# Fused linear-attention and gated-MLP layer: six of the 22 feature tiles of the MLP form their block sums on VectorE instead of by copies into PSUM

## The chip, the core and the metric

One core of a Trainium2 chip runs the whole layer in one launch. The metric is the device time of an execution in microseconds (us), and the lower the better. A kernel's figure is the median of its timed executions; beside it stands one profiled execution, whose trace has the start and duration of every instruction on every engine: TensorE (PE, with its weight loads as PEld), VectorE (DVE), ScalarE (ACT), GpSimd (POOL), and the queues that issue transfers, above all that of SyncE (SP).

## What is computed

The input is x, 2048 tokens of 512 values in float32. After a layer norm, a linear-attention branch and a ReLU-gated MLP branch both read the normalized tokens, and the output joins them. Cut to what matters:

```python
def _B_ref(x, W_gate, W_up, W_down):          # D = 512, F = 1376
    gate = jnp.einsum("bsd,df->bsf", x, W_gate)
    up = jnp.einsum("bsd,df->bsf", x, W_up)
    gate = gate * (gate > 0)
    h = gate * up
    return jnp.einsum("bsf,fd->bsd", h, W_down)

xn = _layernorm(x, axis=-1)
s = _A_ref(xn, A_wqkv, A_w_phi, A_wo)         # 32 heads, feature map by two softmaxes, linear attention
g = _silu(_B_ref(xn, B_W_gate, B_W_up, B_W_down))
return x + s * g
```

The change lies in `gate` and `up` and in how `h` is formed from them.

## The kernel before, in words

**Order of work.** A first phase normalizes and transposes the tokens, projects keys, values and queries and gathers the attention state; it ends at about 167 us of the profile. The rest is two halves. Each half takes 1024 tokens as two blocks of 512, and runs a loop over NF = 11 feature tiles `f` of 128 gate and 128 up features each (line 1203). For each tile `gate_up` (line 559) forms `h` of both blocks, transposed, as 128 features by 512 tokens. `down` (line 633) multiplies `h` by W_down, two tiles at a time (CHUNKS, line 27), and after the last tile come the rest of the down products and the output tiles (`out_tile`, line 896).

**Precision.** Every product of two float32 blocks is made of three matmuls on a high part and a low part of each operand (`mm3`, line 199). With two contraction steps of 128 a product is six matmuls of 128x512 here. `split` (line 194) makes the parts: ScalarE rounds the high part (`hh`), GpSimd subtracts for the low part (`hl`).

**Seven products for eight.** The 2x2 blocks of the tokens are block by contraction half (A11, A12 of the first block, A21, A22 of the second), those of the weights contraction half by gate and up. Winograd's form of Strassen's product needs seven products of sums of blocks. The sums of the tokens (S1 to S4) lie ready in `XT`, those of the weights in `wa`, `wb`, `wc`, `wd`. Call the products P1 = A11·wa0, P2 = A12·wa1, P3 = S4·wd, P4 = A22·wc1, P5 = S1·wc0, P6 = S2·wb0, P7 = S3·wb1. Then the four results are

- gate of the first block: P1 + P2, up of the first block: P1 + P6 + P5 + P3,
- gate of the second block: P1 + P6 + P7 + P4, up of the second block: P1 + P6 + P7 + P5.

**How gate_up adds them.** It issues P1, P7, P6, P2, P5, P4, P3. Sums that share products are carried on in PSUM: ScalarE copies P1 from bank `pa` into bank `pb` (line 565), and TensorE accumulates P6 on top of the copy (line 574); ScalarE copies that sum from `pb` into bank `pd` (line 578), and TensorE accumulates P5 on it (line 588). VectorE adds P7, which ScalarE has copied to `t7`, into `pb` (line 579), forms the second block's up from `pd` and `t7` (line 590), and the two products of gate and up (lines 596 and 601). So P5 can't begin before ScalarE's second copy, and P3 can't begin before VectorE has read `pd` in line 590. After each of the seven products the function yields.

**What stands between the products.** `run` (line 1181) drives the generator. At its second, fourth, sixth and seventh yield (DOWNS, line 41) it issues one step of a pending `down`, if there is one: six or nine matmuls. There is none in tiles 0 and 1 of a half, since the first pair of tiles isn't done, and none in tile 10, since `drain()` (line 1215) has issued the rest ahead of it. In tiles 2 to 9 there always is.

**What sets the order of other work.** `Clock` (line 63) is a planner that lives in the recording of the program: `pace.pump()` issues background work (preparing weights, `q_pair` of the attention queries, which uses VectorE, ScalarE and GpSimd) where its modelled engine times say that it fits. The order recorded is the order on each engine's queue, and each queue is worked off in order. Tiles come from pools: 8 PSUM banks for everything, and 41 buffers of 2 KB for each partition (`u2`) for weights, loads and temporaries; a new tile waits for the last user of the buffer it gets.

**Transfers.** `used(c)` (line 1225) reloads a token block of `XT` for the second half, in the last tile of the first half, as soon as the product that read it is issued. `halfway` reloads `wc`, `wd` and the down weights of the next tile after the third product.

All of the recorded operations carry the line of a helper (L59 in the profile), so the groups are told apart by the names of their tiles: `pa`, `pb`, `pc`, `pd` are the PSUM banks of gate_up; the profile writes `t` for `t7`.

Of the kernel before, what the change touches and what calls it, by code (L numbers as in the profile page):

```python
# [8 lines left out]
F32R = mybir.dt.float32r  # L9
AF = mybir.ActivationFunctionType  # L10
ALU = mybir.AluOpType
AX = mybir.AxisListType

P = 128
# [7 lines left out]
BT = 512  # L22
# [20 lines left out]
A21, A22, A11, A12, S1, S2, S3, S4 = range(8)  # L43
# [116 lines left out]
def layer_kernel(ctx: ExitStack, tc: tile.TileContext, x, wkT, wqT, wv, wo, wf, cst, out):  # L160
    pace = Clock()
    nc = InOrder(tc, pace)
# [4 lines left out]
    def ps(shape=(P, 512), name="ps"):  # L167
        return pp.tile(list(shape), F32, tag="ps", name=name)
# [7 lines left out]
    def u2(shape, name, dt=F32):  # L176
        return sb.tile(list(shape), dt, tag="u2", bufs=B2, name=name)
# [7 lines left out]
    def f32(t):  # L185
        return t.bitcast(F32)

    def add(engine, o, a, b, op=ALU.add):
        engine.tensor_tensor(o, a, b, op=op)

    def mm(o, w, m, start, stop):
        nc.tensor.matmul(o, w, m, start=start, stop=stop, skip_group_check=True)

    def split(hi, lo, src, lo_engine=None):

        nc.scalar.activation(hi, src, AF.Copy)
        add(lo_engine or nc.vector, lo, src, f32(hi), ALU.subtract)

    def mm3(ps_out, w, m, ks, first=True, last=True):

        n = len(ks)
        for i, k in enumerate(ks):
            (wh, wl), (mh, ml) = w(k), m(k)
            mm(ps_out, wl, mh, first and i == 0, False)
            mm(ps_out, wh, ml, False, False)
            mm(ps_out, wh, mh, False, last and i == n - 1)
            if i < n - 1:
                pace.pump()
# [238 lines left out]
    RAW, FT, WD = {}, {}, {}  # L447
# [21 lines left out]
    def w_pair(name):  # L469
        return u2((P, 2, 2, P), name, F32R), u2((P, 2, 2, P), name, F32R)  # L470
# [68 lines left out]
    def f_reload(f, part):  # L539
        if part == 0:  # L540
            FT[f] = [w_pair("wa"), w_pair("wb"), None, None]
            for i, t in enumerate([*FT[f][0], *FT[f][1]]):
                nc.sync.dma_start(f32(flat3(t)), wspill[f][i])
            return
        FT[f][2:] = w_pair("wc"), u2((P, 2, 2, P), "wd", F32R)
        WD[f] = u2((P, D), "fdh", F32R), u2((P, D), "fdl", F32R)
        for i, t in enumerate([*FT[f][2], FT[f][3], *WD[f]]):
            nc.sync.dma_start(f32(flat3(t)), wspill[f][4 + i])

    def w_of(f, i, c=None):  # L550
        t = FT[f][i]
        if c is None:
            return lambda k: (t[:, 0, k, :], t[:, 1, k, :])
        return lambda k: (t[0][:, c, k, :], t[1][:, c, k, :])

    def a_of(c):
        return lambda k: (XT[:, c, 0, k, :], XT[:, c, 1, k, :])

    def gate_up(f, used, halfway):

        pa = ps(name="pa")
        mm3(pa, w_of(f, 0, 0), a_of(A11), range(2))
        used(A11)
        pb = ps(name="pb")
        nc.scalar.activation(pb, pa, AF.Copy)
        last_split()
        yield
        pc = ps(name="pc")
        mm3(pc, w_of(f, 1, 1), a_of(S3), range(2))
        used(S3)  # L570
        t7 = u2((P, BT), "t7")
        nc.scalar.activation(t7, pc, AF.Copy)
        yield
        mm3(pb, w_of(f, 1, 0), a_of(S2), range(2), first=False)
        FT[f][1] = None
        used(S2)
        pd = ps(name="pd")
        nc.scalar.activation(pd, pb, AF.Copy)
        add(nc.vector, pb, pb, t7)
        halfway()  # L580
        yield
        mm3(pa, w_of(f, 0, 1), a_of(A12), range(2), first=False)
        FT[f][0] = None
        used(A12)
        r = u2((P, BT), "r")
        nc.scalar.activation(r, pa, AF.Relu)
        yield
        mm3(pd, w_of(f, 2, 0), a_of(S1), range(2), first=False)
        used(S1)
        add(nc.vector, t7, pd, t7)  # L590
        yield
        mm3(pb, w_of(f, 2, 1), a_of(A22), range(2), first=False)
        FT[f][2] = None
        used(A22)
        h1 = u2((P, BT), "hh", F32R), u2((P, BT), "hl", F32R)
        nc.vector.scalar_tensor_tensor(t7, pb, 0.0, t7, op0=ALU.max, op1=ALU.mult)
        split(*h1, t7, nc.gpsimd)
        yield
        mm3(pd, w_of(f, 3), a_of(S4), range(2), first=False)
        used(S4)  # L600
        add(nc.vector, r, pd, r, ALU.mult)
        h0 = u2((P, BT), "hh", F32R), u2((P, BT), "hl", F32R)
        LATE.append(lambda: split(*h0, r, nc.gpsimd))
        FT.pop(f)
        HS[f] = [h0, h1]
        yield

    HS, Y, LATE = {}, {}, []

    def last_split():  # L610
        while LATE:
            LATE.pop()()
# [566 lines left out]
    pending = []  # L1179

    def run(g, per=1):
        n = 0
        for _ in g:
            pace.pump()
            n += 1
            for _ in range(DOWNS.get(n, 0)):
                if not pending:
                    break
                if next(pending[0], pending) is pending:
                    pending.pop(0)  # L1190
                    if pending:
                        next(pending[0])
                pace.pump()
# [7 lines left out]
    for half in range(2):  # L1201
        b0, b1 = 2 * half, 2 * half + 1
        for f in range(NF):
            if half == 0:
                at[0] = N + f
                pace.finish(preps, lambda: f in DONE)
                if f == 0:
                    queries = pace.add(all_queries(0), 20)
            if half == 1 and f == 0:
                queries = pace.add(all_queries(1), 5)  # L1210
            again = f + 1 < NF and (half or f + 1 in AHEAD)
            if again and f + 1 not in FT:
                f_reload(f + 1, 0)
            if f == NF - 1:
                drain()
                pace.finish(queries)
                for q in QUERIES[half][:4]:
                    if q not in LOADED:
                        o_load(q)
                WO = wo_load()  # L1220
            if f == NF - 2 and not half:
                for q in QUERIES[half][:2]:
                    o_load(q)

            def used(c):
                if half == 0 and f == NF - 1:
                    nc.sync.dma_start(f32(XT[:, c]), xt_spill[:, c - 1])
            run(gate_up(f, used, lambda: again and f_reload(f + 1, 1)))
            for c, fs in enumerate(CHUNKS[:-1]):
                if f == fs[-1]:  # L1230
                    pending.extend(down((b0, b1)[j], j, fs, c == 0) for j in (1, 0))

        last_split()
        drain()
        if half == 0:
            f_reload(0, 0)
            f_reload(0, 1)
        fs = CHUNKS[-1]
        for j, b in enumerate((b1, b0)):
            j = 1 - j  # L1240
            if b == b0:
                for q in QUERIES[half][:2]:
                    o_split(q)
            parts = {}
            for i in range(TPB):
                if j == 1 and i < 3:
                    parts[i] = ps(name="py")
                    down_rows(parts[i], i, j, fs[:-1], True, False)
                    pace.pump()
            for i in range(TPB):  # L1250
                if i in parts:
                    down_rows(parts[i], i, j, fs[-1:], False, True)
                else:
                    parts[i] = ps(name="py")
                    down_rows(parts[i], i, j, fs, True, True)
                y_sum(b, i, parts[i], False, True)
                y = Y[b][:, i, :]
                nc.scalar.activation(y, y, AF.Silu)
                if b * TPB + i in yspill:
                    pace.when(y, lambda t=b * TPB + i, y=y: nc.sync.dma_start(yspill[t], y))  # L1260
                pace.pump()
        for g in fs:
            HS.pop(g), WD.pop(g)
        qs = QUERIES[half]
        for m, q in enumerate(qs):
            if half == 0 and m == 1:
                f_reload(1, 0)
            if m + 2 < len(qs):
                o_split(qs[m + 2])
            if m + 4 < len(qs):  # L1270
                o_load(qs[m + 4])
            for j in range(2):
                out_tile(2 * q + j, WO)
                pace.pump()
# [56 lines left out]
```

## Time and profile before

| | before |
|---|---|
| median of three executions | 564.98 us (564.98 to 565.27) |
| profiled execution | 565.71 us, of which the span of the trace 563.9 us |
| TensorE busy in the span | 556.8 us, 2618 matmuls |
| VectorE, ScalarE, GpSimd busy | 373.4, 312.8, 404.6 us |
| gate_up in tiles 0 and 1, first half | 167.5 to 189.7 us |
| gate_up in tile 10, first half | 315.0 to 324.5 us |
| gate_up in tiles 0 and 1, second half | 357.1 to 377.7 us |
| gate_up in tile 10, second half | 504.6 to 515.4 us |

The profile's matmul rows overlap: a row lasts some 0.39 us, and the next begins before it is over. So TensorE's pace is read from the starts of successive groups of rows, not from durations.

### The profile page before, as it was taken

The numbers are of one execution on the slowest core, as the hardware profiler recorded it, in microseconds if no ns is written. First come the engines' busy times: TensorE is split into PE (matmuls) and PEld (weight loads), VectorE is DVE, ScalarE is ACT, GpSimd is POOL, SyncE is SP. The second block draws the span as 40 slices with busy tenths as digits, with TensorE's granted clock in tenths as the row PEclk, the third lists the DMA queues.
The fourth block names the chain that finished last, engine by engine and source line by source line (L and its number), as shares of the span: only waits on it lengthen the run. The fifth ranks groups of instructions, "written<-read, shape, count | busy, mean of one in ns | idle before, by whom it ended". The sixth has DMA issues, their size and how long they took to land.

```text
span 563.9 us, 8200 instructions
## 1 busy us (share of the span) xinstructions
PE 556.8 (99%) x2618; PEld 465.7 (83%) x2618; DVE 373.4 (66%) x566; ACT 312.8 (55%) x561; POOL 404.6 (72%) x347
## 2 busy tenths in 40 slices
PE   9999999999999999999999999999999999999997
PEld 8898888888888788888888888788888888888886
DVE  5878867677654797699953332679683958764323
ACT  3898787775546567456464251345455555645610
POOL 1689987999888377997988343464568786878473
PEclk9999999999999999999999999999999999999999
DMA  8349989956599817978779999992656765559974
GB/s 271 144 133 260 257 256 305 271 155 176 149 297 317 309 62 263 337 260 293 261 249 341 313 388 410 377 392 57 194 186 200 244 205 158 178 180 314 254 208 166
DMA packets 84539, 137.98 MB, mean 245 GB/s; under 512 B 7824, under 2 KB 34320, under 8 KB 83600
## 3 DMA queue, kind: packets, MB, share of 16 engines
q1 hardware_dynamic: 81040, 125.33, 64.6%
q0 software_dynamic: 3312, 12.06, 11.2%
q8 instruction: 21, 0.34, 0.2%
q14 instruction: 22, 0.18, 0.1%
q10 hardware_dynamic: 144, 0.07, 0.0%
HBM read 76.87 MB, written 52.69 MB: 230 GB/s over the span
## 4 chain that ended last, share of the span: by engine, by line
PE 92%; DVE 3%; DMA 2%; ACT 1%; issue 1%; POOL 0%; SPq 0%; DVEq 0%; ACTq 0%
PE py L59 21%; PE pd L59 10%; PE pa L59 10%; PE pb L59 10%; PE pq L59 8%; PE pso L59 8%; PE pv L59 7%; PE pk L59 7%; PE pc L59 5%; PE pkv L59 3%; PE pnum L59 2%; DMA wvr<-wv 2%; PE pxT L59 1%; DVE eq L59 1%; DMA xt<-x 1%
## 5 line engine op out<-in xcount | busy, mean ns | idle before, releaser
L59 PE MATMUL py<-fdh,hl 128*128 128x512 f32 x176 | 68.5, 389 | 0.0
L59 PE MATMUL py<-fdl,hh 128*128 128x512 f32 x176 | 68.5, 389 | 0.0
L59 PE MATMUL py<-fdh,hh 128*128 128x512 f32 x176 | 68.5, 389 | 0.0
L59 PE MATMUL pa<-XT,wa 128*128 128x512 f32 x264 | 67.2, 389 | 0.0
L59 POOL TENSOR_TENSOR hl<-t,hh 128x512 fp32r<-128x512 f32 x22 | 28.5, 1295 | 50.9 <-ACT hh L59 49.9
L59 PEld LDWEIGHTS pa<-XT,wa 128*128 128x128 f32 x264 | 49.5, 188 | 10.2
L59 DVE TENSOR_TENSOR y<-py,y 128x512 f32<-128x512 f32 x40 | 27.5, 689 | 37.8 <-PE py L59 37.8
L59 DVE TENSOR_TENSOR pb<-pb,t 128x512 f32<-128x512 f32 x22 | 15.3, 697 | 45.9 <-ACT pd L59 45.9
L59 ACT ACTIVATE hh<-t 128x512 fp32r<-128x512 f32 x22 | 13.9, 633 | 53.6 <-DVE t L59 53.6
L59 PE MATMUL pv<-wvh,XT 128*128 128x512 f32 x128 | 43.5, 401 | 0.0
L59 POOL TENSOR_TENSOR phl<-ek,phl 128x1024 fp32r<-128x1024 f32 x15 | 36.1, 2403 | 10.4 <-ACT phl L59 10.4
L59 PE MATMUL pk<-wkh,XT 128*128 128x512 f32 x128 | 42.4, 392 | 0.0
L59 POOL TENSOR_TENSOR ez<-eq,zB 128x1024 f32<-128x1024 f32 x16 | 38.7, 2421 | 3.4 <-ACT eq L59 2.3
L59 PE MATMUL pq<-XT,wqh 128*128 128x512 f32 (+1 forms) x144 | 40.3, 366 | 0.0
L59 POOL TENSOR_TENSOR hl<-r,hh 128x512 fp32r<-128x512 f32 x22 | 28.4, 1292 | 16.1 <-ACT hh L59 14.4
L59 PEld LDWEIGHTS py<-fdh,hh 128*128 128x128 f32 x176 | 33.0, 188 | 6.9
L59 PEld LDWEIGHTS py<-fdl,hh 128*128 128x128 f32 x176 | 33.0, 188 | 6.8
L59 PEld LDWEIGHTS py<-fdh,hl 128*128 128x128 f32 x176 | 33.0, 188 | 6.8
L59 POOL TENSOR_TENSOR y<-y,ys 128x512 f32<-128x512 f32 x24 | 30.9, 1293 | 9.6 <-ACT ys L59 9.6
L59 PE MATMUL pd<-XT,wc 128*128 128x512 f32 x132 | 33.9, 391 | 1.2 <-ACT pd L59 1.2
L59 PE MATMUL pd<-XT,wd 128*128 128x512 f32 x132 | 34.0, 391 | 1.1 <-DVE t L59 1.1
L59 POOL TENSOR_TENSOR ol<-of,oh 128x512 fp32r<-128x512 f32 (+1 forms) x13 | 20.4, 1627 | 20.2 <-ACT oh L59 20.2
(160 smaller groups left out, 1582.2 us busy)
## 6 DMA issues: line engine op xcount, KB each, us to landing
zacc<-ek POOLq DMA_DIRECT2D x15, 512.0 KB, 5.4
xts<-XT SPq DMA_DIRECT2D x4, 1792.0 KB
XT<-xts SPq DMA_DIRECT2D x7, 1024.0 KB, 20.1
wa<-ws SPq DMA_DIRECT2D x26, 256.0 KB, 3.2
wb<-ws SPq DMA_DIRECT2D x26, 256.0 KB, 5.0
wc<-ws SPq DMA_DIRECT2D x26, 256.0 KB, 4.8
ws<-wa SPq DMA_DIRECT2D x22, 256.0 KB, 4.3
ws<-wb SPq DMA_DIRECT2D x22, 256.0 KB, 4.2
```

What stands on the lines that cost most here:

```text
L59: return self.tc.keep_in_program_order(op(*a, **k))
```

## The change

A second function, `gate_up_apart`, is used where no `down` is pending, that is in tiles 0, 1 and 10 of each half, six calls of 22. No product is accumulated on a copy any more. ScalarE copies P1 once, into SBUF (`t1`); the shared sum P1 + P6 is formed by VectorE in SBUF (`u2`, here called m), and VectorE adds it where it is needed. The order of the products becomes P1, P6, P7, P5, P4, P2, P3. Only P4 (on P7, in `pc`), P2 (on P1, in `pa`) and P3 (on P5, in `pd`) are accumulated, each on a product that TensorE wrote.

```diff
+    def gate_up_apart(f, used, halfway):
+        pa = ps(name="pa")
+        mm3(pa, w_of(f, 0, 0), a_of(A11), range(2))
+        used(A11)
+        t1 = u2((P, BT), "t1")
+        nc.scalar.activation(t1, pa, AF.Copy)
+        last_split()
+        yield
+        pb = ps(name="pb")
+        mm3(pb, w_of(f, 1, 0), a_of(S2), range(2))
+        used(S2)
+        m = u2((P, BT), "u2")
+        add(nc.vector, m, pb, t1)
+        yield
+        pc = ps(name="pc")
+        mm3(pc, w_of(f, 1, 1), a_of(S3), range(2))
+        FT[f][1] = None
+        used(S3)
+        halfway()
+        e7 = u2((P, BT), "e7")
+        add(nc.vector, e7, pc, m)
+        yield
+        pd = ps(name="pd")
+        mm3(pd, w_of(f, 2, 0), a_of(S1), range(2))
+        used(S1)
+        add(nc.vector, e7, pd, e7)
+        yield
+        mm3(pc, w_of(f, 2, 1), a_of(A22), range(2), first=False)
+        FT[f][2] = None
+        used(A22)
+        add(nc.vector, pc, pc, m)
+        yield
+        mm3(pa, w_of(f, 0, 1), a_of(A12), range(2), first=False)
+        FT[f][0] = None
+        used(A12)
+        h1 = u2((P, BT), "hh", F32R), u2((P, BT), "hl", F32R)
+        nc.vector.scalar_tensor_tensor(e7, pc, 0.0, e7, op0=ALU.max, op1=ALU.mult)
+        split(*h1, e7, nc.gpsimd)
+        yield
+        mm3(pd, w_of(f, 3), a_of(S4), range(2), first=False)
+        used(S4)
+        add(nc.vector, m, pd, m)
+        nc.vector.scalar_tensor_tensor(m, pa, 0.0, m, op0=ALU.max, op1=ALU.mult)
+        h0 = u2((P, BT), "hh", F32R), u2((P, BT), "hl", F32R)
+        LATE.append(lambda: split(*h0, m, nc.gpsimd))
+        FT.pop(f)
+        HS[f] = [h0, h1]
+        yield
...
-            run(gate_up(f, used, lambda: again and f_reload(f + 1, 1)))
+            run((gate_up if pending else gate_up_apart)(f, used, lambda: again and f_reload(f + 1, 1)))
```

In each of the six calls ScalarE has one copy instead of three copies and a ReLU, and VectorE has five adds and two max-multiplies instead of two adds, one max-multiply and one multiply. TensorE has the same matmuls.

## The prediction

> **What bounds the kernel now.** I read the busy rows and the chain of waits first:
>
> ```profile
> span 563.9 us, 8200 instructions
> PE 556.8 (99%) x2618; PEld 465.7 (83%) x2618; DVE 373.4 (66%) x566; ACT 312.8 (55%) x561; POOL 404.6 (72%) x347
> PE 92%; DVE 3%; DMA 2%; ACT 1%; issue 1%; POOL 0%; SPq 0%; DVEq 0%; ACTq 0%
> ```
>
> TensorE sets the end: 92% of the chain is its own. The change keeps all its matmuls, so it can only take away, add or move moments in which TensorE stands still. Next, therefore, whom TensorE waited for (total us, times, longest), then the starts of its groups around each wait:
>
> ```profile
> PE pd L59 <- ACT pd L59: 1.2, 2, 1.0
> PE pd L59 <- DVE t L59: 1.1, 1, 1.1
> ```
>
> ```profile
> 182.99 1.52 PE L59 MATMUL pa<-XT,wa 128*128 128x512 f32 x6
> 185.47 1.65 PE L59 MATMUL pd<-XT,wc 128*128 128x512 f32 x6 [0.96 <-ACT pd L59]
> 186.96 1.52 PE L59 MATMUL pb<-XT,wc 128*128 128x512 f32 x6
> ...
> 363.92 1.52 PE L59 MATMUL pb<-XT,wc 128*128 128x512 f32 x6
> 366.51 1.66 PE L59 MATMUL pd<-XT,wd 128*128 128x512 f32 x6 [1.07 <-DVE t L59]
> 368.01 1.53 PE L59 MATMUL pa<-XT,wa 128*128 128x512 f32 x6
> 369.37 1.52 PE L59 MATMUL pc<-XT,wb 128*128 128x512 f32 x6
> ...
> 374.81 1.52 PE L59 MATMUL pb<-XT,wc 128*128 128x512 f32 x6
> 377.67 1.52 PE L59 MATMUL pa<-XT,wa 128*128 128x512 f32 x6
> ...
> 508.68 1.52 PE L59 MATMUL pa<-XT,wa 128*128 128x512 f32 x6
> 510.41 1.65 PE L59 MATMUL pd<-XT,wc 128*128 128x512 f32 x6 [0.21 <-ACT pd L59]
> ```
>
> An undisturbed product takes 1.36 us from start to start (368.01 to 369.37). Whatever the starts exceed that by is lost. In tile 1 of the first half: 186.96 - 182.99 - 2.72 = 1.25. In tile 0 of the second half: 368.01 - 363.92 - 2.72 = 1.37. In tile 1: 377.67 - 374.81 - 2.72 = 0.14. In tile 10 of the second half: 510.41 - 508.68 - 1.36 = 0.37, and 0.13 more for the restart that each wait shows (186.96 - 185.47 - 1.36), so 0.50. **Together 3.26 us, all inside the six changed calls.** That is the most the change can give back. What ended two of the waits:
>
> ```profile
> 184.84 0.58 ACT L59 ACTIVATE pd<-pb 128x512 f32<-128x512 f32 x1
> ...
> 365.77 0.68 DVE L59 TENSOR_TENSOR t<-pd,t 128x512 f32<-128x512 f32 x1
> 366.56 0.69 DVE L59 SCALAR_TENSOR_TENSOR t<-pb,t 128x512 f32<-128x512 f32 x1
> ```
>
> In the ScalarE cases the copy into `pd` came late on its queue, and P5 accumulates on it. At 365.77 VectorE's read of `pd` stood behind steps of the attention queries, and P3 writes `pd` next.
>
> From these I take the price of a late releaser. A product due at D whose releaser ends at R loses R - D + 0.18: 365.77 + 0.68 = 366.45 against 365.28 (363.92 + 1.36) gives 1.17, and 1.37 was lost, so 0.20; 184.84 + 0.58 = 185.42 against 184.35 (182.99 + 1.36) gives 1.07 for 1.25, so 0.18.
>
> **The change, part by part.** *ScalarE's copies into PSUM go.* Three of four ScalarE instructions for each call, 18 of some 0.6 us, lie beside TensorE except where the two ScalarE waits name them, and both waits lose their cause: no product needs a ScalarE result any more but P2, which needs the copy of P1 five products earlier. *VectorE gets three more instructions for each call*, 18 in all, every one with one operand in PSUM. Their price has near rows, and so have the steps of the attention queries among which they are queued:
>
> ```profile
> 358.68 1.29 DVE L59 TENSOR_REDUCE mx<-pq 128x32 f32<-128x512 f32 x2
> 359.89 0.68 DVE L59 TENSOR_TENSOR eq<-pq,mx 128x512 f32<-128x512 f32 x1
> ...
> 373.51 0.95 DVE L59 RECIPROCAL qr<-qs 128x128 f32<-128x128 f32 x1
> 374.37 1.16 DVE L59 TENSOR_REDUCE qs<-ez 128x64 f32<-128x1024 f32 x1
> ...
> 376.04 1.21 DVE L59 TENSOR_REDUCE qs<-ez 128x64 f32<-128x1024 f32 x1
> 377.17 0.68 DVE L59 SCALAR_TENSOR_TENSOR t<-pb,t 128x512 f32<-128x512 f32 x1
> 377.76 0.28 DVE L59 TENSOR_TENSOR qs<-qs,qr 128x128 f32<-128x128 f32 x1
> ...
> 379.13 0.68 DVE L59 TENSOR_TENSOR r<-pd,r 128x512 f32<-128x512 f32 x1
> 379.73 2.34 DVE L59 TENSOR_TENSOR eq<-eq,qr 128x1024 f32<-128x1024 f32 x2
> 381.99 0.72 DVE L59 STREAM_TRANSPOSE pq<-pql 128x512 f32<-128x512 f32 x1
> ...
> 511.90 1.52 PE L59 MATMUL pb<-XT,wc 128*128 128x512 f32 x6
> 512.10 0.69 DVE L59 TENSOR_TENSOR t<-pd,t 128x512 f32<-128x512 f32 x1 [1.01 <-PE pd L59]
> ```
>
> An instruction of 128x512 lasts 0.69. The next one starts 0.60 after it (379.13, 379.73), or 0.79 if it needs the result (365.77, 366.56), and the first one starts 0.20 after the end of the product it reads (511.90, 512.10). In the same way a reduction over 1024 is a step of 1.13, a pair over 512 of 1.21, a reciprocal of 0.86, the four small steps behind the last reduction 1.37 (377.76 to 379.13), the pair of scalings 2.26. The 18 new ones make VectorE 10.8 to 12.4 us busier. The operand in PSUM is no new kind (`pd`, `pb` in the rows above), so no wider bounds are needed for the instruction itself.
>
> Of two steps the second starts before the first is over (377.17 with 0.68, then 377.76). The Trainium skill (VectorE: DVE Perf Modes, The DRAIN you can't avoid) says that the next op does not start until the pipe is empty, and adds that an op which isn't held starts earlier. By the strict half each step would be 0.69; the rows bear out the other half, and I count 0.60. What the strict half makes of the time is rival B.
>
> *The new wait.* P4 accumulates in `pc`, so it waits for e7 <- pc + m, with one product (P5) in between. With VectorE free, e7 ends 0.20 + 0.69 = 0.89 after P7, and P4 is due 1.36 after it: nothing is lost while VectorE is less than 0.29 late (0.47 less 0.18). P3 waits for the read of P5 with two products between, and is safer. What is queued behind e7 is the rest of VectorE's list; behind P4, all of TensorE. Call by call:
>
> - *First half, tiles 0 and 10:* VectorE has little else to do; nothing before, nothing after.
> - *First half, tile 1:* VectorE has only the reductions of the attention state beside it, at P6's end, and m follows them before P7 ends at 182.99 (the start of the row `pa<-XT,wa` above, which now is P5's). So e7 runs 183.19 to 183.88, P4 is due at 184.35, and the gain is the full 1.25.
> - *Second half, tile 0:* m waits for the two reductions (359.89) and for P6 (359.84 + 0.20); so m 360.07, two query steps, e7 361.87 to 362.56. P4 is due at 357.12 + 4 x 1.36 = 362.56. Lost 0.18 instead of 1.37. (The tile's other starts are 363.92 less so many times 1.36.)
> - *Second half, tile 1:* it starts at 357.12 + 7 x 1.36 + 0.18 = 366.82, and m when P6 is done, at 366.82 + 2 x 1.36 + 0.20 = 369.74. A reduction follows (370.34), then e7, 371.47 to 372.16; P4 is due at 372.26. Lost 0.08 instead of 0.14.
> - *Second half, tile 2* (unchanged code): VectorE's queue carries the six more steps. From e7 on, each at its start: reduction 372.07, P5 into e7 373.20, reciprocal 373.80, m into `pc` 374.66, reduction 375.26, max-multiply 376.39, P3 into m 376.99, max-multiply 377.78, reduction 378.38, small steps 379.51, scalings 380.88, `pb` 383.14, three transposes 383.74, pair of reductions 385.54, two steps 386.75 and 387.35, and the read of `pd` 387.95 to 388.63. Before it was:
>
> ```profile
> 388.72 0.68 DVE L59 TENSOR_TENSOR t<-pd,t 128x512 f32<-128x512 f32 x1
> 389.91 1.52 PE L59 MATMUL pd<-XT,wd 128*128 128x512 f32 x6
> ```
>
>   Tile 2 starts 1.25 earlier than before (1.19 + 0.06), so P3 is due at 388.66: a new loss of 388.63 - 388.66 + 0.18 = 0.15.
> - *Second half, tile 10:* VectorE is in a transpose when P6 ends:
>
> ```profile
> 507.54 1.24 DVE L59 STREAM_TRANSPOSE ez<-eq 128x1024 f32<-128x1024 f32 x1
> ```
>
>   m 508.70, e7 509.49 to 510.18; P4 is due at 508.68 + 1.36 = 510.04. Lost 0.32 instead of 0.50.
>
> The sum: 1.25 + (1.37 - 0.18) + (0.14 - 0.08) - 0.15 + (0.50 - 0.32) = **2.53 us**. The profiled execution took 565.71 (its span 563.9 and 1.8 around it) and would take 563.2. It lay 0.7 over the median of the runs, 564.98, which would become **562.5**.
>
> *At nothing, GpSimd:* in tile 0 of the second half its difference for h0 now stands ahead of the two `ez` of the queries, not between them:
>
> ```profile
> 371.70 1.29 POOL L59 TENSOR_TENSOR hl<-r,hh 128x512 fp32r<-128x512 f32 x1
> 372.95 2.42 POOL L59 TENSOR_TENSOR ez<-eq,zB 128x1024 f32<-128x1024 f32 x1
> ```
>
> By the walk h0 is done at 369.3; with ScalarE's 0.6 and these two the first `ez` ends at 373.7, and the reduction that reads it comes at 375.26, ahead of the max-multiply for h1 of tile 1. The cover is 1.5; beyond it every us goes to `hl` of h1, which the second down product of tile 2 needs with 0.5 to spare (376.39 + 0.69 + 0.6 + 1.3 and two hand-overs of 0.05, 379.1, against 379.6).
>
> *At nothing, transfers:* `wa` is freed two products later and the `XT` reloads go in another order; the cover is the 33 us between the first half's last product (324.5) and the second half's first (357.1), against
>
> ```profile
> XT<-xts SPq DMA_DIRECT2D x7, 1024.0 KB, 20.1
> ```
>
> Without that cover a reload would cost up to its 20.1. Outside the six calls TensorE's order is the same, instruction by instruction.
>
> **The rivals.** *A, everything comes back:* no new waits, 3.26: 561.7. For it: the walks lose 0.08 to 0.32, about their error. Against: in the second half VectorE's queue has work at each of these places. *B, VectorE's steps don't overlap*, 0.69 for 0.60 and 1.21 for 1.13 each: from m at 369.74 on there are twelve of the one and four of the other before the read of `pd` in tile 2, 1.4 us, which then ends at 390.03. TensorE is there 390.03 + 0.18 - 389.91 = 0.30 behind its old place, where the forecast has it 1.10 ahead: 1.25 - 0.30 + 0.18 = 1.13, so 563.9. For it: the new steps hang on products more often than those of the rows. Against: the rows. (It is the strict half of the Trainium skill's VectorE: DVE Perf Modes, The DRAIN you can't avoid.)
>
> *C, the gain is taken back later:* the time gained in tile 1 runs into a place without slack:
>
> ```profile
> 279.44 0.68 DVE L59 TENSOR_TENSOR t<-pd,t 128x512 f32<-128x512 f32 x1
> 280.35 1.54 PE L59 MATMUL pd<-XT,wd 128*128 128x512 f32 x6
> ```
>
> VectorE's read ends at 280.12, 0.01 before the weight load that belongs to the matmul of 280.35 would be due. If the work ahead of that read doesn't move with TensorE, because GpSimd or a transfer sets it, the 1.25 is lost again: 563.7. Against: VectorE's list there begins with results that come from the products of the tile before, through ScalarE and GpSimd, which move along. *D, slower:* VectorE becomes the bound of the second half's first three tiles. Its idle time there is waits for products:
>
> ```profile
> 356.90:377.70 20.80, 19.73 (x87) 15.83 (x86) 16.64 (x23) 9.07 (x13) 9.38 (x6) 1.00 1.03 385
> ```
>
> It was busy 16.64 of 20.80. If none of the rest can be used, the six steps make the read of `pd` in tile 2 later than its old 388.72 by 6 x 0.60 = 3.6, of which 389.91 - 0.18 - 389.40 = 0.33 was slack: 1.25 + 0.18 + 0.33 - 3.6 = -1.8, so 566.8. It decides from 1.8 us of lateness on; my walk has the read 0.8 early. *That the change doesn't do what it says* I leave out: the new function is taken wherever no `down` is pending, and VectorE's list in the changed program has just 18 more instructions, ScalarE's 18 fewer.
>
> **How the numbers follow.** Forecast 0.55 (561.9 to 563.4: each walk is good to some 0.3), A 0.12, B 0.13, C 0.10, D 0.10. A measurement of this kernel can tell 0.2%, 1.1 us, from no change, so faster ends at 563.85: that is the forecast, A, and something over a third of B and C, which lie at the border: 0.76. Within 0.2% 0.15, slower (D, less the part of it that uses some idle time) 0.09. The range goes from A to 0.7 beyond B, for B's and C's own errors and a mild form of D: 561.6 to 564.6.
>
> **What would show it.** In the profile after: no TensorE wait for ScalarE's `pd`; groups from `pa` to `pd` 1.36 apart in tile 1 of the first half; waits for VectorE under 0.4 at P4 (`pc`) in the second half's tiles 0, 1 and 10 and at P3 (`pd`) in tile 2; VectorE some 11 us busier, ScalarE some 11 less. It is wrong if TensorE waits for VectorE more than 1 us at one place, for GpSimd's `hl` or a transfer at all, or if the place at 280 takes the 1.25 back.

## The result, and the profile after

The changed kernel took 563.25 us (median of 7 runs, 562.88 to 563.52), the kernel before, on the same chip, 564.98 (7 runs, 564.72 to 565.27): a ratio of 0.9969, with a 95% interval of 0.9958 to 0.9981. That is 1.73 us less (1.1 to 2.4). Forecast were 2.5 less, 562.5, in a range of 561.6 to 564.6.

The profiled executions lie 2.83 apart (565.71 and 562.88), more than the medians: the first lay 0.73 above its median, the second 0.37 below. The rest is a lead of 1.08 that the second already has where its first `gate_up` begins (166.42 for 167.50), behind the same instructions in the same order. The first experiment shows that it belongs to those two executions and not to the change.

The page of the kernel after: the span, the busy time of each engine, and the chain of waits by engine.

```profile
span 561.1 us, 8197 instructions
...
PE 555.5 (99%) x2618; PEld 465.0 (83%) x2618; DVE 386.2 (69%) x584; ACT 303.1 (54%) x543; POOL 404.6 (72%) x347
...
PE 93%; DVE 3%; DMA 2%; issue 0%; SPq 0%; POOL 0%
```

VectorE is 12.8 us busier (386.2 for 373.4; forecast were 10.8 to 12.4, and 0.5 of it is `qd`, of which more below), ScalarE 9.7 less. TensorE still makes 93% of the chain. The view of waits of the kernel after (who waited for whom, total us, times, longest):

```profile
PEld pc L59 <- DVE e L59: 1.1, 3, 0.4
...
PE pd L59 <- DVE t L59: 0.5, 1, 0.5
```

No product waits for ScalarE's `pd` any more. Three short waits for e7 (`e`) at P4 (`pc`), and one for VectorE's read (`t`) at a P3 (`pd`), 0.46 long in the row below where the prediction named 0.4 as the most. Now the starts of TensorE's groups around each place, in the timeline of the kernel after:

```profile
181.23 0.84 PE L59 MATMUL pc<-XT,wb 128*128 128x512 f32 x3
181.91 1.52 PE L59 MATMUL pd<-XT,wc 128*128 128x512 f32 x6
183.27 1.52 PE L59 MATMUL pc<-XT,wc 128*128 128x512 f32 x6
...
358.86 1.52 PE L59 MATMUL pd<-XT,wc 128*128 128x512 f32 x6
360.30 1.66 PE L59 MATMUL pc<-XT,wc 128*128 128x512 f32 x6
361.79 1.52 PE L59 MATMUL pa<-XT,wa 128*128 128x512 f32 x6
...
368.59 1.52 PE L59 MATMUL pd<-XT,wc 128*128 128x512 f32 x6
370.05 1.66 PE L59 MATMUL pc<-XT,wc 128*128 128x512 f32 x6
371.55 1.52 PE L59 MATMUL pa<-XT,wa 128*128 128x512 f32 x6
...
383.79 1.52 PE L59 MATMUL pb<-XT,wc 128*128 128x512 f32 x6
...
387.13 1.66 PE L59 MATMUL pd<-XT,wd 128*128 128x512 f32 x6 [0.46 <-DVE t L59]
388.62 0.40 PE L59 MATMUL py<-fdh,hl 128*128 128x512 f32 x1
...
506.06 1.52 PE L59 MATMUL pd<-XT,wc 128*128 128x512 f32 x6
507.58 1.66 PE L59 MATMUL pc<-XT,wc 128*128 128x512 f32 x6
509.08 1.52 PE L59 MATMUL pa<-XT,wa 128*128 128x512 f32 x6
```

Read as in the prediction, by what the starts exceed 1.36 for each product:

- *First half, tile 1.* P5 begins when the last three matmuls of P7 are issued (181.23 + 0.68), P4 follows 1.36 later. Nothing is lost; the 1.25 is back in full.
- *Second half, tile 0:* 361.79 - 358.86 - 2.72 = 0.21 (forecast 0.18, before 1.37).
- *Tile 1:* 371.55 - 368.59 - 2.72 = 0.24 (forecast 0.08, before 0.14).
- *Tile 2:* between P4 and P3 stand six matmuls of `down`, which take as long as a product; so 387.13 - 383.79 - 2.72 = 0.62, and the restart 388.62 - 387.13 - 1.36 = 0.13. Together **0.75** (forecast 0.15, before 0).
- *Tile 10:* 509.08 - 506.06 - 2.72 = 0.30 (forecast 0.32, before 0.50).

That is 1.50 lost where 3.26 was: 1.76 gained by the trace, 1.73 by the medians. Of the 0.77 by which the forecast was too good, 0.60 lie in tile 2. VectorE's rows of the kernel after show why; the small steps behind the last reduction are those from 377.33 to 379.35.

```profile
358.37 0.68 DVE L59 TENSOR_TENSOR eq<-pq,mx 128x512 f32<-128x512 f32 x1
358.97 0.68 DVE L59 TENSOR_TENSOR eq<-mx,pq 128x512 f32<-128x512 f32 x1
359.56 0.68 DVE L59 TENSOR_TENSOR e<-pc,u 128x512 f32<-128x512 f32 x1
...
367.58 0.69 DVE L59 TENSOR_TENSOR u<-pb,t 128x512 f32<-128x512 f32 x1 [0.67 <-ACT hh L59]
...
377.33 0.29 DVE L59 TENSOR_TENSOR qs<-qs,qr 128x128 f32<-128x128 f32 x1
377.65 0.74 DVE L59 SCALAR_TENSOR_TENSOR qd<-qs 128x64 f32<-128x64 f32 x1
378.43 0.55 DVE L59 RECIPROCAL qd<-qd 128x64 f32<-128x64 f32 x1
379.02 0.30 DVE L59 TENSOR_TENSOR qr<-qr,qd 128x128 f32<-128x128 f32 x1
379.35 2.35 DVE L59 TENSOR_TENSOR eq<-eq,qr 128x1024 f32<-128x1024 f32 x2
...
386.40 0.67 DVE L59 TENSOR_TENSOR t<-pd,t 128x512 f32<-128x512 f32 x1
```

The walk had those steps at 1.37; here they took 379.35 - 377.33 = 2.02. One instruction makes the difference: `qd`, the sum of the two softmax denominators (line 736 of the kernel before), took 0.74, and in the row of the kernel before at this place 0.23:

```profile
378.08 0.23 DVE L59 SCALAR_TENSOR_TENSOR qd<-qs 128x64 f32<-128x64 f32 x1
...
378.92 0.30 DVE L59 TENSOR_TENSOR qr<-qr,qd 128x128 f32<-128x128 f32 x1
```

What is new beside it is on GpSimd. In the kernel after, the low part for h0 of tile 1 runs until 378.32, and `qd` ends 0.07 later:

```profile
377.03 1.29 POOL L59 TENSOR_TENSOR hl<-u,hh 128x512 fp32r<-128x512 f32 x1
```

In the kernel before GpSimd stood idle there, from 375.37 to the start of this row:

```profile
378.66 1.29 POOL L59 TENSOR_TENSOR hl<-t,hh 128x512 fp32r<-128x512 f32 x1 [3.29 <-ACT hh L59]
```

So the theory with which the experiments begin: the losses at each call are what the stalls of VectorE's list make of them, and in tile 2 the list is later than forecast because `qd` is held by GpSimd.

### The profile page after: what moved, and what is told of

The parts are those of the page before. It is cut to its first block, busy times and chain, and to the rows that moved or that the text cites. A ratio compares the mean times of both kernels' runs of the same rounds, so it can differ in the third digit from the quotient of the medians.

```text
span 561.1 us, 8197 instructions
## 1 busy us (share of the span) xinstructions
PE 555.5 (99%) x2618; PEld 465.0 (83%) x2618; DVE 386.2 (69%) x584; ACT 303.1 (54%) x543; POOL 404.6 (72%) x347
## 4 chain that ended last, share of the span: by engine, by line
PE 93%; DVE 3%; DMA 2%; issue 0%; SPq 0%; POOL 0%
PE py L59 21%; PE pd L59 10%; PE pa L59 9%; PE pb L59 8%; PE pv L59 8%; PE pk L59 8%; PE pq L59 8%; PE pso L59 8%; PE pc L59 6%; PE pkv L59 3%; PE pnum L59 3%; PE pxT L59 1%; PE pfold L59 1%; DMA pql<-pq 1%; DMA wd<-ws 1%; DVE eq L59 1%
## 5 line engine op out<-in xcount | busy, mean ns | idle before, releaser
L59 POOL TENSOR_TENSOR hl<-t,hh 128x512 fp32r<-128x512 f32 x16 | 20.8, 1298 | 27.3 <-ACT hh L59 26.3
L59 PE MATMUL pc<-XT,wb 128*128 128x512 f32 x132 | 33.7, 389 | 0.0
L59 PE MATMUL pb<-XT,wb 128*128 128x512 f32 x132 | 33.5, 389 | 0.0
L59 POOL TENSOR_TENSOR pTl<-ez,pTh 128x1024 fp32r<-128x1024 f32 x10 | 24.0, 2400 | 8.4 <-ACT pTh L59 8.4
```

The lines of the kernel that those rows point to most:

```text
L59: return self.tc.keep_in_program_order(op(*a, **k))
```

## The experiments

Every experiment was timed in rounds with the kernel before, whose medians were 565.21 (e1 to e4), 565.09 (e5 to e8) and 565.23 (e9 to e12); a gain is counted from the median of the same rounds. The table has what each lost at the five places, read from the starts in its trace as above (first half tile 1; second half tiles 0, 1, 2 and 10), what that makes of the 3.26 lost before, and the difference of the medians.

| kernel | tile 1, first | 0 | 1 | 2 | 10 | gain by trace | gain by medians | ratio, 95% |
|---|---|---|---|---|---|---|---|---|
| changed kernel | 0 | 0.21 | 0.24 | 0.75 | 0.30 | 1.76 | 1.73 | 0.9958 to 0.9981 |
| e1 | 0 | 1.37 | 0.14 | 0 | 0.50 | 1.25 | 1.32 | 0.9969 to 0.9987 |
| e2 | 1.27 | 0.21 | 0.45 | 0 | 0.51 | 0.82 | 0.76 | 0.9977 to 0.9995 |
| e3 | 1.27 | 0.21 | 0.14 | 0.76 | 0.52 | 0.36 | 0.38 | 0.9985 to 1.0003 |
| e4 | 0 | 0.21 | 0.45 | 0 | 0.30 | 2.30 | 2.60 | 0.9946 to 0.9971 |
| e5 | 0 | 0.21 | 0.23 | 0.42 | 0.03 | 2.37 | 2.35 | 0.9945 to 0.9970 |
| e6 | 0 | 0.21 | 1.26 | 0.75 | 0.29 | 0.75 | 0.69 | 0.9976 to 0.9994 |
| e7 | 0 | 0 | 0 | 1.02 | 0 | 2.24 | 2.15 | 0.9950 to 0.9975 |
| e8 | 0 | 0 | 0.63 | 0 | 0 | 2.63 | 2.43 | 0.9941 to 0.9968 |
| e9 | 0 | 0.21 | 0.24 | 1.37 | 0.30 | 1.14 | 1.24 | 0.9971 to 0.9988 |
| e10 | 0 | 0 | 0 | 0.81 | 0 | 2.45 | 2.54 | 0.9941 to 0.9966 |
| e11 | 0 | 0.21 | 0.47 | 0 | 0 | 2.58 | 2.85 | 0.9937 to 0.9962 |
| e12 | 1.23 | 1.36 | 0.14 | 0 | 0.22 | 0.31 | 0.61 | 0.9981 to 0.9999 |

The two columns of gains agree within 0.3 in all thirteen rows, though the places differ from row to row. So these five places account for what these changes do; the one loss outside them, 0.30 in e7, is told there. The intervals are 1 to 1.5 us wide, so kernels that lie closer than that are told apart by their traces, not by their times.

### Which calls pay (e1 to e4)

Each is the changed kernel with another condition in the line that chooses the function:

```diff
-            run((gate_up if pending else gate_up_apart)(f, used, ...))
+            run((gate_up_apart if not pending and half == 0 else gate_up)(f, used, ...))                     # e1
+            run((gate_up_apart if half == 1 and f == 0 else gate_up)(f, used, ...))                          # e2
+            run((gate_up_apart if half == 1 and f < 2 else gate_up)(f, used, ...))                           # e3
+            run((gate_up_apart if not pending and not (half == 1 and f == 1) else gate_up)(f, used, ...))    # e4
```

e1, the first half alone:

> The new function is used in the first half only (tiles 0, 1, 10). Theory (each call pays for itself where its stall was): the 1.25 us of tile 1 and nothing else, so 564.98 - 1.25 = 563.7; in the second half TensorE waits as before: some 1.1 for VectorE's t at P3 of tile 0, and for ScalarE's pd in tile 10. Rival (the 1.08 us by which the changed kernel's profiled execution began its first gate_up earlier, 166.42 for 167.50, belong to the change and not to that one execution): 1.25 + 1.08, so 562.7.

Measured: 563.89, a gain of 1.32. The theory holds; the rival's 2.33 lies outside the interval (0.7 to 1.8).

e2, tile 0 of the second half alone:

> The new function is used in tile 0 of the second half only. Theory (tile 2's new loss comes from the three extra VectorE instructions of tile 1, since VectorE's list behind its add for P6 of tile 1 is released by that product and moves along with TensorE): 1.37 - 0.21 = 1.16 gained, none lost later, so 563.8; no wait for VectorE's t at P3 of tile 2. Rival (any gain in TensorE ahead of tile 2 runs into VectorE's list there, which stays where it was): P3 is due 1.16 earlier and loses 389.40 - 388.75 + 0.18 = 0.83 again, so 564.65, with a wait of some 0.7 at P3 of tile 2.

Measured: 564.45, a gain of 0.76, between the two; the interval (0.3 to 1.3) holds both, so the trace has to decide. Tile 2 loses nothing, as the theory has it, but something is lost one tile earlier than the rival had it, at P3 of tile 1:

```profile
373.26 1.52 PE L59 MATMUL pb<-XT,wc 128*128 128x512 f32 x6
374.94 1.65 PE L59 MATMUL pd<-XT,wd 128*128 128x512 f32 x6 [0.15 <-DVE t L59]
376.43 1.52 PE L59 MATMUL pa<-XT,wa 128*128 128x512 f32 x6
```

376.43 - 373.26 - 2.72 = 0.45, where 0.14 was lost before. VectorE's rows of the same kernel tell what is late:

```profile
371.49 0.70 DVE L59 TENSOR_TENSOR pb<-pb,t 128x512 f32<-128x512 f32 x1 [1.49 <-ACT pd L59]
372.10 1.21 DVE L59 TENSOR_REDUCE qs<-eq 128x64 f32<-128x1024 f32 x1
```

In this list a reduction of `eq` stands behind the add for P6 of tile 1 (`pb<-pb,t`) and ahead of the read of P5, for which P3 waits. In the kernel before both stood ahead of that add, in time that was idle:

```profile
368.88 2.33 DVE L59 TENSOR_REDUCE qs<-eq 128x64 f32<-128x1024 f32 x2
```

The planner counts VectorE's work when it places the steps of the queries; that the three more instructions of tile 0 moved this one is likely, and wasn't tried apart.

e3, tiles 0 and 1 of the second half:

> The new function is used in tiles 0 and 1 of the second half only. Theory (tile 1's three extra VectorE instructions cost more in tile 2 than they save): 1.16 gained in tile 0, 0.10 lost in tile 1, 0.75 lost in tile 2, so 564.98 - 0.31 = 564.7, slower than with tile 0 alone, with a wait of some 0.5 for VectorE's t at P3 of tile 2. Rival (the loss in tile 2 needs what the first half's calls moved, or was of that one execution): 1.06 gained, so 563.9, and no such wait.

Measured: 564.83, a gain of 0.38, with 0.76 lost in tile 2 without any change in the first half. By the traces that is less than e2's gain (0.36 for 0.82), as the theory had it; the intervals of the two times overlap. The rival's 1.06 lies outside the interval, which ends at 0.85.

e4, all but tile 1 of the second half:

> The new function in all of its six calls but tile 1 of the second half. Theory (that call alone loses, in itself and in tile 2): 1.25 + 1.16 + 0.20 = 2.61 gained, so 562.4, 0.85 below the changed kernel's 563.25; no wait at P3 of tile 2. Rival (the gain so far runs into VectorE's list in tile 2 whatever tile 1 does): the loss in tile 2 stays, 563.1 to 563.3.

Measured: 562.61, a gain of 2.60; no wait in tile 2. The interval (1.6 to 3.1) just reaches the rival's 1.7 to 1.9, so it is the missing wait that decides against it. One call of the six costs more than it brings: with it tiles 1 and 2 lose 0.24 + 0.75, without it 0.45 + 0. That leaving it out gives about the gain that was forecast for all six is chance: the losses lie at other places.

### What holds qd (e5, e12)

```diff
-        r = ps((P, 2, 64), name="qr")
+        qn = ps((P, 3, 64), name="qr")
+        r, even = qn[:, 0:2], qn[:, 2].rearrange("p (j h) -> p j h", j=2)
...
-        nc.vector.tensor_tensor(sums[:, 1], sums[:, 1], r, op=ALU.mult)
-        part = sums[:, 1].rearrange("p j (h s) -> p j h s", s=2)
-        nc.vector.scalar_tensor_tensor(den, part[:, :, :, 0], 1e-6, part[:, :, :, 1], op0=ALU.add, op1=ALU.add)
+        part, rs = (t.rearrange("p j (h s) -> p j h s", s=2) for t in (sums[:, 1], r))
...
+        nc.vector.tensor_tensor(even, part[:, :, :, 0], rs[:, :, :, 0], op=ALU.mult)
+        nc.vector.tensor_tensor(part[:, :, :, 1], part[:, :, :, 1], rs[:, :, :, 1], op=ALU.mult)
+        nc.vector.scalar_tensor_tensor(den, even, 1e-6, part[:, :, :, 1], op0=ALU.add, op1=ALU.add)
...
```

The lines left out tell the planner the costs of the old instructions, so that the order of all others stays.

> The changed kernel, with the sum for qd reading one operand from PSUM and one from SBUF instead of both from SBUF; for that the product ahead of it is made in two instructions of half the size, so VectorE has eight more instructions. Theory (qd is held until the GpSimd instruction beside it is over, because both of its inputs lie in SBUF): all eight qd last 0.2 to 0.3 (now 0.22 to 0.77, median 0.70), GpSimd's instructions are as long as before, and the read of pd in tile 2 ends some 0.25 earlier (0.51 less for qd, some 0.25 for the added instruction), so the loss in tile 2 falls from 0.75 to some 0.5 and the time to 563.0. Rival (qd waits for a result or a hand-over, not for the port): its length stays at 0.5 to 0.8, and the loss grows to some 1.0: 563.5.

Measured: 562.74, a gain of 2.35 over the kernel before, where the changed kernel has 1.73. The group of `qd` in the changed kernel, and in this one (count, then shortest, median and longest duration in ns):

```profile
L59 DVE SCALAR_TENSOR_TENSOR qd<-qs x8: 224/698/766, 202.6 to 500.5; 128x64 f32<-128x64 f32 x8
```

```profile
L59 DVE SCALAR_TENSOR_TENSOR qd<-qr,qs x8: 223/224/226, 203.1 to 500.7; 128x64 f32<-128x64 f32 x8
```

All eight are short now, also the one in question, which runs while GpSimd works as before (VectorE's and GpSimd's rows of this kernel):

```profile
378.18 0.23 DVE L59 SCALAR_TENSOR_TENSOR qd<-qr,qs 128x64 f32<-128x64 f32 x1
```

```profile
377.37 1.28 POOL L59 TENSOR_TENSOR hl<-u,hh 128x512 fp32r<-128x512 f32 x1
```

Its other operand is still written by the instruction just ahead of it. So neither a late input nor the signal between two instructions made `qd` long, but its second operand in SBUF. Tile 2 loses 0.42 for 0.75, about the step forecast (0.25; it was 0.33). The 0.27 that came back in tile 10 I hadn't expected: there too a `qd` lies ahead, in the list that holds the add of P6 up.

e12, the same edit in the kernel before:

> The kernel before with qd reading one operand from PSUM. Theory (a VectorE list that is not late anywhere behind a qd gains nothing from a shorter one): the eight qd fall to 0.23, and the time stays within 0.2 of 564.98; the TensorE waits at P3 of tile 0 and for ScalarE's pd are as they were. Rival (the qd cost time in many places): 0.3 to 0.6 less, as in the changed kernel.

Measured: 564.62, a gain of 0.61 (0.1 to 1.1). The lengths fell as expected, but my expectation of no gain was wrong. TensorE's rows in tile 10 of this kernel:

```profile
508.21 1.52 PE L59 MATMUL pa<-XT,wa 128*128 128x512 f32 x6
509.67 1.65 PE L59 MATMUL pd<-XT,wc 128*128 128x512 f32 x6
511.15 1.54 PE L59 MATMUL pb<-XT,wc 128*128 128x512 f32 x6
```

511.15 - 508.21 - 2.72 = 0.22 was lost where it had been 0.50. The chain there runs from VectorE's list over ScalarE to the copy into `pd`: VectorE's transposes behind `qd` end at 508.04 (508.78 in the kernel before), ScalarE's instruction that reads them (`pTh`) starts at 508.07 (508.81), and its copy into `pd` behind that at 509.03 (509.78). So a held `qd` was paid for in the kernel before as well. The other 0.3 of the medians is not located; the interval holds 0.31.

### VectorE's list in tile 2 (e6, e9)

One add of 128x512 is put into tile 1 of the second half, its result unused; e6 reads `pd`, e9 reads `pc`:

```diff
         add(nc.vector, pc, pc, m)
+        if half == 1 and f == 1:
...
+            add(nc.vector, t1, pd, t1)      # e6; in e9: add(nc.vector, t1, pc, t1)
...
```

The lines left out keep the add from the planner.

> The changed kernel with one more VectorE add of 128x512 in tile 1 of the second half (after the add of P4, reading pd, its result unused). Theory (from there to the read of pd in tile 2 VectorE's list has no idle time, so the read is late by every step put in): P3 of tile 2 loses 0.75 + 0.60 = 1.35, with a wait of some 1.1, and the time is 563.85. Rival (the list has slack, and the 0.75 comes from a wait in it for GpSimd or ScalarE): the loss stays at 0.75 and the time at 563.25.

Measured: 564.40, a gain of only 0.69. The place was not the expected one:

```profile
372.12 1.54 PE L59 MATMUL pa<-XT,wa 128*128 128x512 f32 x6
374.36 1.67 PE L59 MATMUL pd<-XT,wd 128*128 128x512 f32 x6 [0.69 <-DVE t L59]
375.87 1.32 PE L59 MATMUL pa<-XT,wa 128*128 128x512 f32 x5
```

P3 of tile 1 writes `pd`, so it had to wait for the added read: 375.87 - 372.12 - 2.72 = 1.03. TensorE then came to tile 2 later, as did the list, and lost its 0.75 there as before. The experiment had put a wait of its own into the kernel, and says nothing on the theory. e9 mends that:

> The changed kernel with one more VectorE add of 128x512 at the same place as in the run before it of this kind, but reading pc, which a later VectorE instruction reads anyway, so that no product waits for the added one (its result is unused). Theory (VectorE's list between that add and the read of pd in tile 2 has no idle time): no wait at P3 of tile 1; P3 of tile 2 loses 0.75 + 0.60 = 1.35, a wait of some 1.05, and the time is 563.85. Rival (the list has slack there): the loss stays at 0.75, the time at 563.25.

Measured: 563.99, a gain of 1.24, 0.5 less than the changed kernel's. TensorE's rows and the one new wait in this stretch:

```profile
376.14 1.52 PE L59 MATMUL pc<-XT,wb 128*128 128x512 f32 x6
...
378.99 1.53 PE L59 MATMUL pb<-XT,wb 128*128 128x512 f32 x6
...
384.44 1.52 PE L59 MATMUL pb<-XT,wc 128*128 128x512 f32 x6
...
388.27 1.65 PE L59 MATMUL pd<-XT,wd 128*128 128x512 f32 x6 [0.95 <-DVE t L59]
```

```profile
PEld py L59 <- POOL hl L59: 0.3, 1, 0.3
```

P3 of tile 2 loses 388.27 - 384.44 - 2.72 = 1.11 and the restart of 0.13. The remaining 0.13 is lost ahead of 378.99 (2.85 after 376.14), where the down product waits for GpSimd's `hl`: the max-multiply for h1 stands in the same list, and the half us that the prediction gave as spare is used up. In sum 1.37 for 0.75: one step of 0.60 costs TensorE 0.62. The list between tile 1 and the read in tile 2 has no slack.

### Two products between P7 and P4 (e7), and the edits together (e8, e10, e11)

```diff
+        if half == 1:
+            mm3(pa, w_of(f, 0, 1), a_of(A12), range(2), first=False)
+            FT[f][0] = None
+            used(A12)
+            yield
         mm3(pc, w_of(f, 2, 1), a_of(A22), range(2), first=False)
         FT[f][2] = None
         used(A22)
         add(nc.vector, pc, pc, m)
-        yield
-        mm3(pa, w_of(f, 0, 1), a_of(A12), range(2), first=False)
-        FT[f][0] = None
-        used(A12)
+        if half == 0:
+            yield
+            mm3(pa, w_of(f, 0, 1), a_of(A12), range(2), first=False)
+            FT[f][0] = None
+            used(A12)
```

> The changed kernel with P2 issued ahead of P4 in its three calls of the second half, so that two products lie between P7 and P4. Theory: the losses at P4 (0.21, 0.24 and 0.30) go, since e7 <- pc + m now has 1.36 more; VectorE's list in tile 2 doesn't move, so P3 of tile 2 takes back up to 0.45 of it: 563.25 - 0.30 = 562.95, a loss of up to 1.2 at P3 of tile 2, and no TensorE wait at pc. Rival (the list moves along with TensorE): 563.25 - 0.75 = 562.5. The planner places some background work of the second half elsewhere in this kernel, for which I allow 0.3 either way.

Measured: 562.94, a gain of 2.15. The three losses at P4 are gone, and P3 of tile 2 takes part of it back:

```profile
384.18 1.52 PE L59 MATMUL pb<-XT,wc 128*128 128x512 f32 x6
...
387.79 1.66 PE L59 MATMUL pd<-XT,wd 128*128 128x512 f32 x6 [0.73 <-DVE t L59]
```

387.79 - 384.18 - 2.72 + 0.13 = 1.02, so 0.27 of the 0.75 came back there. Between theory and rival, nearer the theory.

One loss of this trace lies outside the five places: 0.30 in the first half, at the place that rival C named. P3 there starts at 278.79, 0.22 late, and loses 0.08 more in the restart. Up to there the engines have the same instructions in the same order as in the changed kernel. But ScalarE's `woh` waited 1.47 for a transfer (`wor`, landed by 258.36) where it waited 0.70 in the changed kernel; VectorE's list, which at 260.94 waits for ScalarE's `pTh`, is 0.27 later from there on, and its read of `pd` ends at 278.64, when P3 was due at 278.57. With it the gain by trace is 1.94. Whether other executions of this kernel lose it too is not known.

e8 has this order and tile 1 of the second half in the old form:

> P2 ahead of P4 in the second half, and tile 1 of the second half in the old form. Theory: as the kernel without tile 1 (a gain of 2.6), and 0.30 more in tile 10; the 0.21 of tile 0 is lost again at P3 of tile 1, where VectorE's list was already late: a gain of 2.9 over the kernel before, 562.1, 1.1 below the changed kernel. Rival (the list of tile 1 moves along): a gain of 3.1, 561.9. Rival (the shifted background work costs more than the 0.3): no better than the kernel without tile 1.

Measured: 562.66, a gain of 2.43, no better than e4 by the medians. Its trace has nothing lost in tiles 0, 2 and 10, and 0.63 at P3 of tile 1, 0.18 more than e4: what tile 0 no longer loses is lost there, as the theory has it. By the trace it is 0.33 ahead of e4; the timing can't tell that.

e10 has all six calls, this order, and e5's edit:

> All six calls, P2 ahead of P4 in the second half, and qd with one operand in PSUM. Theory: only P3 of tile 2 still loses, 1.02 - 0.33 = 0.7 of the 3.26, so a gain of 2.55 over the kernel before: 562.4. Rival (with P2 ahead VectorE's list is set by the products, so the shorter qd buys nothing): the loss in tile 2 stays at 1.0, 562.75.

Measured: 562.69, a gain of 2.54, as forecast; the loss in tile 2 is 0.81, 0.21 less than in e7, and nothing is lost at e7's place in the first half.

e11 is e4 with e5's edit:

> The new function in all calls but tile 1 of the second half, and qd with one operand in PSUM. Theory: losses of 0.21 (tile 0), 0.45 (P3 of tile 1), nothing in tile 2 and 0.03 in tile 10 instead of 0.30: a gain of 3.26 - 0.69 = 2.57 by the traces, 562.3 to 562.4, 0.25 below the same kernel with qd as it was. Rival (no qd lies ahead of a wait here): 562.6.

Measured: 562.38, a gain of 2.85 (2.1 to 3.6), the lowest of all. It beats the kernel before clearly. The changed kernel's gain, 1.73 (1.1 to 2.4), was measured in other rounds and its interval overlaps; by the traces e11 is 0.8 ahead of it. From e4, e8 and e10 the timing doesn't tell it apart. What is still lost in it is 0.21 at P4 of tile 0 and 0.47 at P3 of tile 1.

## Why the prediction was right, and where it was not

- **Where the time lay: right.** All of it was in the six calls and in what follows them. The 3.26 of stalls is the ceiling: no kernel here gained more, and the losses at five places add up to every result within 0.3.
- **The sum: too high.** 2.53 lies just above the measured interval (1.1 to 2.4), and 563.25 near the upper end of the band that the forecast gave itself (561.9 to 563.4). By the traces 0.77 is missing, 0.60 of it in tile 2.
- **First half, tile 1: right in size.** 1.25 forecast; 1.25 by e1's trace, 1.32 by its median.
- **The new wait at P4: right.** P4 waits for e7 at the three places named, with 0.21, 0.24 and 0.30 for 0.18, 0.08 and 0.32. In tile 1 the walk was 0.16 too good: m began at 367.58, 0.35 after P6 ended (368.59 - 1.36 = 367.23) instead of 0.20. The profile puts that down to ScalarE's rounding of `hh`, which ended at 367.58; it was not tested.
- **The new loss in tile 2: right in place and mechanism, wrong in size.** This is the step that failed: "a new loss of 388.63 - 388.66 + 0.18 = 0.15" measured 0.75. The price held, R - D + 0.18 with R = 386.40 + 0.67 = 387.07 and D = 383.79 + 2.72 = 386.51 gives 0.74. R was off. The walk had the read end at 388.63, which is 386.29 on the clock of the new trace (P5 of tile 0 began at 358.86, the walk had 357.12 + 3 x 1.36 = 361.20, so all of it lies 2.34 earlier), and it ended at 387.07. Of these 0.78, 0.16 were there when the small steps began (377.33 for 379.51 - 2.34), as in tile 1, and 0.65 came in them, less 0.03 afterwards. Of the 0.65, 0.51 is `qd` (0.74 for 0.23) and 0.12 the step behind `qr`, on which the scalings wait directly now (379.35 - 379.02, for 379.13 - 378.92). D was 0.19 later than forecast, from tiles 0 and 1. The mistake of method: I took the four small steps as 1.37 from one row of a place where GpSimd stood idle, and moved the list to a place where it didn't. The prediction looked at GpSimd for what it must deliver, not for what it holds up. The other rows of `qd` in the trace of before, up to 0.76 long, would have said so.
- **Rival A** (everything comes back): fell; 1.50 of 3.26 is lost again. e7 and e11 show that it could be made nearly true place by place.
- **Rival B** (VectorE's steps don't overlap): fell. In the rows above, 358.37, 358.97, 359.56, instructions of 0.68 start 0.60 apart in the new list too, so the strict half of the Trainium skill's rule (VectorE: DVE Perf Modes, The DRAIN you can't avoid) isn't borne out here. The time lies about midway between the forecast and B's 563.9, but the difference was not lost by B's mechanism.
- **Rival C** (the place at 280 takes 1.25 back): fell for the changed kernel. No wait for that read stands in the view of waits, and e1 kept its gain to the end. But the place has as little slack as the prediction said: in e7's profiled execution a transfer that landed later made it lose 0.30, by C's mechanism.
- **Rival D** (VectorE is the bound of three tiles): fell as a forecast of slower, but its direction was seen: in tiles 1 and 2 the list is without slack (e9), and there each added step costs its full length. By the traces of e2 and e3, tile 1's call alone turns a gain of 0.82 into 0.36.
- **Transfers and GpSimd's deliveries: right.** No TensorE wait for either; the spare of `hl` was real, since one more step (e9) used it up.

## What to carry over

Work that is moved onto an engine off the critical path costs nothing where that engine's list has idle time ahead of the next result that is waited for, and its full length where it hasn't: decide it call by call, from the list between the added step and the next wait. When a list is walked forward, a duration from a row holds only with the same neighbours on the other engines; look at all instances of the instruction and at what ran beside the short and the long ones. And when an added instruction is to measure slack, it must read nothing that a later write waits for.

## What the hardware showed beyond expectation

A VectorE instruction with both inputs in SBUF (`qd`) stood still until the GpSimd instruction beside it was over. Of the sixteen `qd` in the traces of before and after three lasted 0.22 to 0.23, all while GpSimd was idle. The other thirteen lasted 0.49 to 0.77, and each ended 0.07 to 0.09 after the end of a GpSimd instruction that had begun before it. An instance of the kernel before, on VectorE and on GpSimd:

```profile
439.69 0.69 DVE L59 SCALAR_TENSOR_TENSOR qd<-qs 128x64 f32<-128x64 f32 x1
```

```profile
439.02 1.29 POOL L59 TENSOR_TENSOR hl<-t,hh 128x512 fp32r<-128x512 f32 x1 [0.99 <-ACT hh L59]
```

439.69 + 0.69 = 440.38, and 439.02 + 1.29 = 440.31. With one of the two operands in PSUM (e5) all eight are short; seven of them began while a GpSimd instruction ran, and GpSimd's own busy time is the same (404.8 for 404.6). The traces of before and after hold a second control: `pTl<-peT,pTh`, a VectorE instruction of 128x512 with `peT` in PSUM, began beside a running GpSimd instruction all 24 times and always lasted 0.67 to 0.70. The Trainium skill (SBUF — State Buffer, Who interferes with whom) states that a VectorE instruction with two SBUF inputs contends with a GpSimd instruction that reads SBUF, and, of the pair of ports that the two share, that whoever issues first has it for the whole instruction while the other fully blocks. The runs agree where VectorE comes second, with the numbers here; GpSimd coming second no run here shows. By that rule `qd` is held in tile 2 until 377.03 + 1.29 = 378.32, and its row ends 0.07 later. The prediction didn't weigh it.
